# Turning the next pair's inputs inside this pair's product, in the MLP's accumulator ring

## The chip, the core and the metric

The kernel runs on one core of a Trainium2 chip. The metric is the device time of one execution in microseconds (us), the median of several runs. Before the change it is 194.65 us (three runs, 194.28 to 195.99).

The core has five engines that work side by side and wait for each other by semaphores: TensorE (matrix products and transposes, which write to PSUM, the accumulator memory), VectorE, ScalarE, GpSimd, and SyncE, which issues most transfers here. In the profile they are PE (and PEld for its weight loads), DVE, ACT, POOL and SP.

## The reference

Two stages. The first is a linear attention with decay (RWKV-5): for each of 4 batches and 8 heads a state of 48 x 48 is carried through 768 time steps. The second is an MLP with a SiLU.

```python
batch, n_heads, seq, head_dim = (4, 8, 768, 48)
for t in range(S):
    cur = np.einsum('bhd,bhe->bhde', u[None] * kt, vt)
    y[:, :, t] = np.einsum('bhd,bhde->bhe', rt, state + cur)
    state = w[None, :, :, None] * state + np.einsum('bhd,bhe->bhde', kt, vt)
# x: y as (3072, 384)
h = x @ w_in                         # 384 -> 2048
g = h * (1.0 / (1.0 + np.exp(-h)))
return (g @ w_out)                   # 2048 -> 384
```

All inputs and the output are fp32.

## The kernel before

The time axis is cut into six chunks of 128 steps. A *unit* is one chunk of one batch: 24 units, unit `i` being chunk `i // 4` of batch `i % 4`, handled in pairs `i`, `i + 1`. For each unit:

- r and k are turned (transposed) by TensorE in fp32, so that the head's 48 channels lie on the partitions, and VectorE multiplies them with powers of the decay on the way out of PSUM (`turn`, `decay`): this gives `rT` and `kT`;
- the product of `kT` and `rT` (fp32) gives a 128 x 128 matrix per head, which VectorE masks to its triangle (`masked`: `am`, fp16);
- `outputs`: `am` times v, plus `rT` times the carried state, gives `y`; k times v gives the new contribution to the state;
- `y` is evicted, turned by a DMA transpose into `xT`, and becomes input of the MLP.

The MLP is cut into small pieces, called fillers, which stand in a list and are put into TensorE's stream between the attention's steps by `fill(n)`. A piece of the first layer (`l1`) is three matmuls with 512 columns into one accumulator `hps` and a SiLU on ScalarE; a piece of the second layer (`l2`) is four matmuls with 384 columns; four such pieces fill one accumulator `ops`, which ScalarE then copies out. A chunk has 16 pieces of each layer.

PSUM holds two large tiles `att0` and `att1` (two banks each), taken in turn by the transposes and by the products, and a ring of four one-bank accumulators (tag `moe`) for everything else: `hps`, `ops`, `yp` (outputs), `sp` (state).

```python
wrk = ctx.enter_context(tc.tile_pool(name="wrk", bufs=2))
att = [ps.tile([128, 2, 512], FP, name=f"att{i}") for i in range(2)]
# ... cut ...
def turn_one(i, x):
    if x == 0:
        L(i)["t"] = next_att().rearrange("p y (x g t) -> p y x g t", x=2, g=NP)
    flat = (rin, kin)[x][i % NIN].rearrange("p h d -> p (h d)")
    for p in range(NP):
        for y in range(2):
            rows = slice(HC * y, HC * y + HC)
            nc.tensor.transpose(L(i)["t"][0:PR, y, x, p, :], flat[rows, 128 * p:128 * p + PR],
                                ident[rows, rows])

def decay_one(i, x):
    key, lam = (("rT", lamR), ("kT", lamK))[x]
    L(i)[key] = wrk.tile([PR, NP, C], FP, name=key)          # pool of two buffers
    nc.vector.tensor_tensor(
        out=L(i)[key].rearrange("p g (y t) -> p y g t", y=2),
        in0=L(i)["t"][0:PR, :, x], in1=lam.rearrange("p g (y t) -> p y g t", y=2),
        op=ALU.mult)

def product_pair(i):
    a = [next_att().rearrange("p j (g c) -> p j g c", g=NP) for _ in range(2)]
    for e in range(2):
        L(i + e)["a"] = a[e]
    for s0, c0 in ((0, 0), (HC, HC)):
        for p in range(NP):
            for e in range(2):
                rT, kT = L(i + e)["rT"], L(i + e)["kT"]
                o0 = s0 if e == 0 else HC - s0
                for j, r0 in ((0, 0), (1, 64)):
                    nc.tensor.matmul(a[e][o0:o0 + HC, j, p, c0:C],
                                     kT[r0:r0 + D, p, s0:s0 + HC],
                                     rT[r0:r0 + D, p, c0:C], start=True, stop=True)
# ... cut ...
def l1_mm(sc, b0, nb, ft):
    m = B // nb
    hps = hpss[b0, ft] = ps.tile([128, m, nb * C], FP, name="hps", tag="moe", bufs=4)
    # three matmuls; then a SiLU on ScalarE

def l2_mm(sc, b, part):
    if part == 0:
        opss[b] = ps.tile([128, HD], FP, name="ops", tag="moe", bufs=4)
    # four matmuls; after part 3 a copy on ScalarE and the store
# ... cut: the head, in which the first units and MLP pieces are ordered by hand ...
load(8)
load(9)
for i in range(B + 2, NU, 2):                # B = 4, NU = 24: i = 6, 8 ... 22
    nxt = range(i + 2, min(i + 4, NU))
    product_pair(i)
    # ... cut: GpSimd's products for the next pair ...
    masked(i)
    masked(i + 1)
    fill(4)
    outputs(i)
    # ... cut: evict y, DMA transpose, state ...
    fill(2)
    outputs(i + 1)
    # ... cut: the same, and new fillers after every second pair ...
    fill(2)
    for n in nxt:
        turn(n)
        decay(n)
    load(i + B)
    load(i + 1 + B)
    for n in nxt:
        bonus_sum(n); cast_v(n); bonus_v(n); decayed_state(n)
    for n in nxt:
        fill(2)
        cast_r(n)
    fill(4)
fill(len(fillers))
```

Of the kernel before, what the change touches and what calls it, by code (L numbers as in the profile page):

```python
# [8 lines left out]
FP = mybir.dt.float32  # L9
F16 = mybir.dt.float16  # L10
AF = mybir.ActivationFunctionType
ALU = mybir.AluOpType
# [3 lines left out]
def kernel(  # L16
# [11 lines left out]
    nc = tc.nc  # L28

    B, H, S, D = r.shape  # L30
    C = 128
    NCH = S // C
    HD = H * D
    NP = H // 2
    PW = 2 * D
    PR = 64 + D
# [4 lines left out]
    NIN = 8  # L41
    HC = C // 2
# [3 lines left out]
    wrk = ctx.enter_context(tc.tile_pool(name="wrk", bufs=2))  # L46
    ps = ctx.enter_context(tc.tile_pool(name="ps", bufs=1, space=bass.MemoryType.PSUM))
    ctx.enter_context(tc.manual_schedule())

    def unit(i):  # L50
        return divmod(i, B)
# [4 lines left out]
    def next_att():  # L56
        turns.append(0)
        return att[len(turns) % 2]
# [3 lines left out]
    rin = [big.tile([128, H, 64], FP, name=f"rin{i}") for i in range(NIN)]  # L62
    kin = [big.tile([128, H, 64], FP, name=f"kin{i}") for i in range(NIN)]
# [7 lines left out]
    def ld(i, dst, src, eng=nc.sync):  # L71
        sc, b = unit(i)
        eng.dma_start(
            out=dst[i % NIN][:, :, 0:D],
            in_=src[b, :, sc * C:sc * C + C, :].rearrange("h t d -> t h d"))

    def load(i):
        if i >= NU:
            return
        for dst, src in ((rin, r), (kin, k), (vin, v)):  # L80
            ld(i, dst, src)
# [38 lines left out]
    for b in range(B):  # L120
        nc.vector.memset(st16[b], 0.0)

    ident = cst.tile([128, 128], FP)
# [10 lines left out]
        out=maskM, in_=maskM, compare_op=ALU.is_ge, fill=0.0,  # L134
# [11 lines left out]
    lamR = cst.tile([PR, NP, C], FP)  # L146
    lamK = cst.tile([PR, NP, C], FP)
# [54 lines left out]
    def L(i):  # L202
        return live.setdefault(i, {})

    def bonus_products(i):
        bonus_ku(i)
        bonus_rku(i)
# [10 lines left out]
    def decayed_k(i):  # L218
        nc.gpsimd.tensor_tensor(out=kc[i % NIN][:, :, 0:D], in0=kin[i % NIN][:, :, 0:D],  # L219
                                in1=lamC, op=ALU.mult)  # L220

    def bonus_sum(i):
        L(i)["rku"] = wrk.tile([128, H], FP, name="rku")
        nc.vector.tensor_reduce(out=L(i)["rku"], in_=L(i)["rku_f"],  # L224
                                axis=mybir.AxisListType.X, op=ALU.add)

    def bonus_v(i):
        L(i)["vu"] = wrk.tile([128, H, D], FP, name="vu")
        nc.gpsimd.tensor_tensor(out=L(i)["vu"], in0=vin[i % NIN],  # L229
                                in1=L(i)["rku"].unsqueeze(2).broadcast_to([128, H, D]),  # L230
                                op=ALU.mult)

    def crossed(i):
        return i % 2 == 1
# [9 lines left out]
# [12 lines that stand above are left out]
        L(i)[key] = wrk.tile([PR, NP, C], FP, name=key)  # L256
# [5 lines that stand above are left out]
    def turn(i):  # L262
        turn_one(i, 0)
        turn_one(i, 1)

    def decay(i):
        decay_one(i, 0)
        decay_one(i, 1)
# [3 lines left out]
        nc.scalar.copy(out=L(i)["rT16"], in_=L(i)["rT"])  # L272

    def product_pair(i):
        a = [next_att().rearrange("p j (g c) -> p j g c", g=NP) for _ in range(2)]
        for e in range(2):
            L(i + e)["a"] = a[e]
        for s0, c0 in ((0, 0), (HC, HC)):
            for p in range(NP):
                for e in range(2):  # L280
                    rT, kT = L(i + e)["rT"], L(i + e)["kT"]
                    o0 = s0 if e == 0 else HC - s0
                    for j, r0 in ((0, 0), (1, 64)):
                        nc.tensor.matmul(a[e][o0:o0 + HC, j, p, c0:C],  # L284
                                         kT[r0:r0 + D, p, s0:s0 + HC],
                                         rT[r0:r0 + D, p, c0:C],
                                         start=True, stop=True)

    def masked(i):
        am = L(i)["am"] = wrk.tile([128, 2, NP, C], F16, name="am")  # L290
        nc.vector.tensor_tensor(  # L291
            out=am.rearrange("p h g c -> p (h g) c"), in0=L(i)["a"].rearrange("p h g c -> p (h g) c"),
            in1=(maskX if crossed(i) else maskM).unsqueeze(1).broadcast_to([128, H, C]), op=ALU.mult)
# [27 lines left out]
    def outputs(i):  # L321
        outputs_y(i)
        outputs_s(i)

    def decayed_state(i):
        sc, b = unit(i)
        if 0 < sc < NCH - 1:
            L(i)["sdec"] = wrk.tile([PR, NP, PW], FP, name="sdec", bufs=4)
            nc.gpsimd.tensor_tensor(out=L(i)["sdec"], in0=st[b],  # L329
                                    in1=wCT.unsqueeze(2).broadcast_to([PR, NP, PW]), op=ALU.mult)  # L330

    def evict_y(i):
        L(i)["y16"] = wrk.tile([128, H, D], F16, name="y16")
        nc.vector.tensor_tensor(out=L(i)["y16"], in0=L(i)["y"], in1=L(i)["vu"], op=ALU.add)  # L334

    def state(i):
        sc, b = unit(i)
        if sc == NCH - 1:
            return
        sps = L(i)["sps"]  # L340
        for p0, c0 in ((0, 0), (64, D)):
            dst = st[b][p0:p0 + D, :, c0:c0 + D]
            src = sps[p0:p0 + D, :, c0:c0 + D]
            if sc:
                nc.vector.tensor_tensor(out=dst, in0=src,
                                        in1=L(i)["sdec"][p0:p0 + D, :, c0:c0 + D], op=ALU.add)
            else:
                nc.vector.tensor_copy(out=st16[b][p0:p0 + D, :, c0:c0 + D], in_=src)
                nc.vector.tensor_copy(out=dst, in_=src)
# [13 lines left out]
    def turn_y_dma(i):  # L363
        sc, b = unit(i)
        nc.sync.dma_start_transpose(out=x_tile(sc)[:, :, b, :],
                                    in_=L(i)["y16"].rearrange("p h d -> p (h d)"))
# [31 lines left out]
    def l1(sc, b0, nb, ft):  # L398
        l1_mm(sc, b0, nb, ft)
        l1_silu(sc, b0, nb, ft)  # L400
# [22 lines left out]
            store(sc, b)  # L423

    fillers = []

    def fill(n):
        for _ in range(n):
            if fillers:
                fillers.pop(0)()  # L430
# [45 lines left out]
    for word in order.split():  # L476
        if "*" in word:
            n, word = word.split("*")
# [10 lines left out]
            l1(1, 0, 2, 2 * int(word[1]))  # L489
        else:  # L490
            unit_steps[word[:-1]](int(word[-1]))
    load(8)
    load(9)
    fillers.extend([lambda ft=ft: l1(1, 0, 2, ft) for ft in range(10, NFT, 2)])
    fillers.extend(second(0))

    for i in range(B + 2, NU, 2):
        sc, b = unit(i)
        nxt = range(i + 2, min(i + 4, NU))
        product_pair(i)  # L500
        if i > B + 2:
            for n in nxt:
                bonus_products(n)
                decayed_k(n)
        if i > B + 2:
            masked(i)
            masked(i + 1)
        else:
            bonus_v(i)
            decayed_k(i)  # L510
            decayed_state(i)
            masked(i)
            bonus_sum(i + 1)
            masked(i + 1)
            bonus_v(i + 1)
            decayed_k(i + 1)
            decayed_state(i + 1)
            for n in nxt:
                bonus_products(n)
                decayed_k(n)  # L520
        fill(4)
        outputs(i)
        evict_y(i)
        turn_y_dma(i)
        state(i)
        state16(i)
        fill(2)
        outputs(i + 1)
        evict_y(i + 1)
        turn_y_dma(i + 1)  # L530
        state(i + 1)
        state16(i + 1)
        if b:
            fillers.extend((first(sc) if sc > 1 else rest_first(sc)) + second(sc))
        fill(2)
        for n in nxt:
            turn(n)
            decay(n)
        load(i + B)
        load(i + 1 + B)  # L540
        for n in nxt:
            bonus_sum(n)
            cast_v(n)
            bonus_v(n)
            decayed_state(n)
        for n in nxt:
            fill(2)
            cast_r(n)
        fill(4)
    fill(len(fillers))  # L550


# [28 lines left out]
```

## Time and profile before

The profiled execution has a span of 195.2 us. In the groups below a line such as L284 is a line of the kernel; then come the engine, the operation, the tiles (written <- read), the shape and how many there are, the busy time and the mean of one instruction.

| what | engine | number | mean |
|---|---|---|---|
| product `att<-rT,kT` (L284) | TensorE, fp32 | 768 | 258 ns |
| first layer `hps<-xT,win` (L387) | TensorE, fp16 | 360 | 337 ns |
| second layer `ops<-wout,gT` (L408) | TensorE, fp16 | 384 | 326 ns |
| decay `rT<-att,lamR`, `kT<-att,lamK` (L257) | VectorE | 24 + 24 | 685 and 683 ns |
| mask `am<-att` (L291) | VectorE | 12 + 12 | 1225 and 1215 ns |
| SiLU `gT<-hps` (L395) | ScalarE | 96 | 598 ns |
| cast `rT<-rT` (L272) | ScalarE | 20 | 619 ns |

Matmuls overlap in TensorE's pipeline, so their mean is a latency; what one costs in a stream is the distance between starts. Each product matmul is recorded twice[...]. Transposes are the instructions of L251.

### The profile page before, as it was taken

How to read it: one execution, taken by the hardware profiler on the slowest of the kernel's cores; microseconds unless marked ns; L12 is line 12 of the kernel's file. 1: busy time of each engine (PE TensorE's matmuls, PEld its weight loads, DVE VectorE, ACT ScalarE, POOL GpSimd, SP SyncE). 2: the span in 40 equal slices, each digit the busy share in tenths (PEclk: the TensorE clock that was granted, in tenths of full speed). 3: DMA queues.
4: the chain of work that ended last, by engine and by line, in shares of the span. 5: the costliest groups of instructions: out<-in, count | busy, mean ns of one | idle time of the engine just before them, and what ended most of it. 6: DMA issues, size and time to landing. Idle time of an engine off the chain costs nothing.

```text
span 195.2 us, 5592 instructions
## 1 busy us (share of the span) xinstructions
PE 186.8 (96%) x2290; PEld 119.4 (61%) x2290; DVE 102.9 (53%) x188; ACT 108.2 (55%) x211; POOL 120.3 (62%) x159
## 2 busy tenths in 40 slices
PE   7998999889999999999999999999999999999992
PEld 2565676567766786665556655566655657644561
DVE  6348869783862772782782673663564364200121
ACT  5394558749563384076793186791386781089200
POOL 8567994999999948919919829839837430000000
PEclk9999999999999999999999999999999999999999
DMA  5999999999748639258349269168287201310022
GB/s 95 210 205 179 201 167 176 172 211 190 109 100 164 186 75 232 69 113 177 90 95 211 64 146 195 30 125 181 61 185 162 43 1 44 95 66 0 6 78 81
DMA packets 90123, 24.35 MB, mean 125 GB/s; under 512 B 83313, under 2 KB 90098, under 8 KB 90098
## 3 DMA queue, kind: packets, MB, share of 16 engines
q1 hardware_dynamic: 84992, 20.46, 48.1%
q0 software_dynamic: 3712, 3.15, 11.1%
q10 hardware_dynamic: 1394, 0.40, 0.8%
q8 instruction: 18, 0.29, 0.7%
q14 instruction: 7, 0.06, 0.1%
HBM read 20.65 MB, written 4.72 MB: 130 GB/s over the span
## 4 chain that ended last, share of the span: by engine, by line
PE 75%; POOL 13%; issue 4%; DMA 2%; ACT 2%; DVE 1%; ACTq 0%; POOLq 0%
PE ops L408 32%; PE hps L387 26%; PE att L284 7%; PE att L251 4%; POOL ku L211 3%; POOL kc L219 3%; POOL vu L229 2%; DMA u_bc<-in_u_dram 2%; POOL rku_f L215 2%; PE yp L306 2%; PE yp L301 2%; POOL win L84 2%; PE sp L318 1%; ACT gT L395 1%; POOL sdec L329 0%
## 5 line engine op out<-in xcount | busy, mean ns | idle before, releaser
L387 PE MATMUL hps<-xT,win 128*128 128x512 f16 (+1 forms) x360 | 68.2, 337 | 0.7 <-ACT xT L376 0.5
L395 ACT ACTIVATE gT<-hps 128x512 f16<-128x512 f32 x96 | 56.2, 598 | 19.9 <-PE hps L387 17.8
L408 PE MATMUL ops<-wout,gT 128*128 128x384 f16 x384 | 66.6, 326 | 0.0
L408 PEld LDWEIGHTS <-gT 128*128 128x128 f16 x384 | 36.2, 98 | 23.2
L387 PEld LDWEIGHTS <-win 128*128 128x128 f16 x360 | 33.2, 98 | 24.2 <-issue 1.1
L229 POOL TENSOR_TENSOR vu<-vin,rku 128x384 f32<-128x384 f32 x24 | 19.8, 830 | 29.9 <-DVE rku L224 29.9
L414 ACT COPY osb<-ops 128x384 f32<-128x384 f32 x20 | 9.6, 479 | 43.4 <-PE ops L408 43.4
L291 DVE TENSOR_TENSOR am<-att,maskM 128x1024 f16<-128x1024 f32 x12 | 14.7, 1225 | 35.0 <-PE att L284 35.0
L211 POOL TENSOR_TENSOR ku<-kin,u_bc 128x384 f32<-128x384 f32 x24 | 24.1, 1005 | 3.5 <-DMA u_bc<-in_u_dram 2.3
L215 POOL TENSOR_TENSOR rku_f<-rin,ku 128x384 f32<-128x384 f32 x24 | 24.1, 1003 | 1.7
L219 POOL TENSOR_TENSOR kc<-kin,lamC 128x384 f16<-128x384 f32 x24 | 23.9, 1000 | 0.0
L284 PEld LDWEIGHTS att<-rT,kT 48*64 48x64 f32 x768 | 18.9, 141 | 6.5 <-issue 3.9
L257 DVE TENSOR_TENSOR rT<-att,lamR 112x512 f32<-112x512 f32 x24 | 16.4, 685 | 11.5 <-ACT gT L395 4.0
L284 PE MATMUL att<-rT,kT 48*64 48x128 f32 (+1 forms) x768 | 21.4, 258 | 0.8 <-DVE rT L257 0.8
L334 DVE TENSOR_TENSOR y<-yp,vu 128x384 f16<-128x384 f32 x24 | 13.3, 556 | 13.7 <-issue 4.8
L257 DVE TENSOR_TENSOR kT<-att,lamK 112x512 f32<-112x512 f32 x24 | 16.4, 683 | 3.6 <-PE att L251 3.5
L291 DVE TENSOR_TENSOR am<-att,maskX 128x1024 f16<-128x1024 f32 x12 | 14.6, 1215 | 0.0
L416 DVE COPY osb<-ops 128x384 f32<-128x384 f32 x4 | 2.2, 558 | 21.8 <-PE ops L408 21.8
L329 POOL TENSOR_TENSOR sdec<-st,wCT 112x384 f32<-112x384 f32 x16 | 13.2, 826 | 0.0
L238 ACT CAST v<-vin 128x384 f16<-128x384 f32 x24 | 11.4, 511 | 3.2 <-DMA vin<-in_v_dram 3.2
L224 DVE TENSOR_REDUCE rku<-rku_f 128x8 f32<-128x384 f32 x24 | 12.4, 544 | 0.8 <-POOL rku_f L215 0.7
L272 ACT CAST rT<-rT 112x512 f16<-112x512 f32 x20 | 12.4, 619 | 0.3 <-DVE rT L257 0.2
(60 smaller groups left out, 167.0 us busy)
## 6 DMA issues: line engine op xcount, KB each, us to landing
rin<-in_r_dram SPq DMA_DIRECT2D x24, 192.0 KB, 4.1
vin<-in_v_dram SPq DMA_DIRECT2D x24, 192.0 KB, 3.9
out_dram<-osb SPq DMA_DIRECT2D x24, 192.0 KB, 2.2
kin<-in_k_dram SPq DMA_DIRECT2D x23, 192.0 KB, 4.1
win<-in_moe_w_in_dram POOLq DMA_DIRECT2D x4, 384.0 KB, 6.3
wout<-in_moe_w_out_dram POOLq DMA_DIRECT2D x4, 384.0 KB, 6.5
xT<-y SPq DMA_TRANSPOSE x18, 2.3
kin<-in_k_dram ACTq DMA_DIRECT2D x1, 192.0 KB, 3.7
```

The costliest lines, as they stand in the source:

```text
L211: nc.gpsimd.tensor_tensor(out=L(i)["ku"], in0=kin[i % NIN][:, :, 0:D], in1=u_bc, op=ALU.mult)
L215: nc.gpsimd.tensor_tensor(out=L(i)["rku_f"], in0=rin[i % NIN][:, :, 0:D], in1=L(i)["ku"], op=ALU.mult)
L219: nc.gpsimd.tensor_tensor(out=kc[i % NIN][:, :, 0:D], in0=kin[i % NIN][:, :, 0:D], in1=lamC, op=ALU.mult)
L229: nc.gpsimd.tensor_tensor(out=L(i)["vu"], in0=vin[i % NIN], in1=L(i)["rku"].unsqueeze(2).broadcast_to([128, H, D]), op=ALU.mult)
L257: nc.vector.tensor_tensor(out=L(i)[key].rearrange("p g (y t) -> p y g t", y=2), in0=L(i)["t"][0:PR, :, x], in1=lam.rearrange("p g (y t) -> ...
L284: nc.tensor.matmul(a[e][o0:o0 + HC, j, p, c0:C], kT[r0:r0 + D, p, s0:s0 + HC], rT[r0:r0 + D, p, c0:C], start=True, stop=True)
L291: nc.vector.tensor_tensor(out=am.rearrange("p h g c -> p (h g) c"), in0=L(i)["a"].rearrange("p h g c -> p (h g) c"), in1=(maskX if crossed ...
L329: nc.gpsimd.tensor_tensor(out=L(i)["sdec"], in0=st[b], in1=wCT.unsqueeze(2).broadcast_to([PR, NP, PW]), op=ALU.mult)
L334: nc.vector.tensor_tensor(out=L(i)["y16"], in0=L(i)["y"], in1=L(i)["vu"], op=ALU.add)
L387: nc.tensor.matmul(hps[:, f, :], win[:, q, (ft + f) * 128:(ft + f + 1) * 128], xts[sc][:, q, b0:b0 + nb, :].rearrange("p b t -> p (b t)"), ...
L395: nc.scalar.activation(out=gts[sc][:, ft:ft + m, b0 * C:(b0 + nb) * C], in_=hpss[b0, ft], func=AF.Silu)
L408: nc.tensor.matmul(opss[b], gts[sc][:, ft, b * C:(b + 1) * C], wout[:, ft, :], start=(ft == 0), stop=(ft == NFT - 1))
```

## The change

The loop's pairs from `i = 8` on take another order.

- The transposes of the next pair stand between the two halves of this pair's product, so that product and transposes form one stretch of fp32 work on TensorE.
- They no longer use `att0` and `att1`, which the product occupies, but all four accumulators of the MLP's ring: each unit's transposes go to two tiles, one for each half of the chunk's 128 steps (`turn_halves`), and the decays become four per unit with half the elements each (`decay_halves`).
- The decays stand before the masks in VectorE's order.
- The number of MLP pieces of each pair is set by a table: 8 and 24 in turn in place of 16 (15 in the first, 16 in the second, 20 in the next to last). The pieces around the transposes are then those of the second layer, which take one ring buffer for four pieces.
- Loads run two units further ahead.

```diff
+    def turn_halves(i):
+        L(i)["th"] = [ps.tile([128, 512], FP, name="th", tag="moe", bufs=4)
+                      .rearrange("p (x g t) -> p x g t", x=2, g=NP) for _ in range(2)]
+        for x in range(2):
+            flat = (rin, kin)[x][i % NIN].rearrange("p h d -> p (h d)")
+            for p in range(NP):
+                for y in range(2):
+                    rows = slice(HC * y, HC * y + HC)
+                    nc.tensor.transpose(L(i)["th"][y][0:PR, x, p, :],
+                                        flat[rows, 128 * p:128 * p + PR], ident[rows, rows])
+
+    def decay_halves(i):
+        for key in ("rT", "kT"):
+            L(i)[key] = wrk.tile([PR, NP, C], FP, name=key)
+        for y in range(2):
+            for x, (key, lam) in enumerate((("rT", lamR), ("kT", lamK))):
+                t0 = HC * y
+                nc.vector.tensor_tensor(
+                    out=L(i)[key][:, :, t0:t0 + HC], in0=L(i)["th"][y][0:PR, x],
+                    in1=lam[:, :, t0:t0 + HC], op=ALU.mult)
... cut: product_pair split into open_products and products(i, s0) ...
+    STEPS = {6: 15, 8: 16, 10: 8, 12: 24, 14: 8, 16: 24, 18: 8, 20: 20, 22: 8}
...
-    load(8)
-    load(9)
+    for i in range(8, 12):
+        load(i)
...
-        product_pair(i)
-        if i > B + 2:
+        ahead = i > B + 2
+        if ahead:
+            open_products(i)
+            products(i, 0)
+            for n in nxt:
+                turn_halves(n)
+            products(i, HC)
             for n in nxt:
                 bonus_products(n)
                 decayed_k(n)
-        if i > B + 2:
+            for n in nxt:
+                decay_halves(n)
             masked(i)
             masked(i + 1)
+            fill(6)
         else:
+            product_pair(i)
... cut: the first pair keeps its order and its fill(4) ...
-        fill(2)
-        for n in nxt:
-            turn(n)
-            decay(n)
-        load(i + B)
-        load(i + 1 + B)
+        if not ahead:
+            fill(2)
+            for n in nxt:
+                turn(n)
+                decay(n)
+        load(i + 6)
+        load(i + 7)
... cut ...
+        left = STEPS[i] - 8
         for n in nxt:
-            fill(2)
+            if left > 4:
+                fill(2)
+                left -= 2
             cast_r(n)
-        fill(4)
+        fill(left)
```

It is meant to save TensorE one change between fp16 and fp32 work and back in every pair, and to take the decays out of the stretch behind the outputs.

More of the change, by code (lines that the diff above doesn't have):

```diff
@@ L274, in product_pair, with open_products @@
     def product_pair(i):
-        a = [next_att().rearrange("p j (g c) -> p j g c", g=NP) for _ in range(2)]
+        open_products(i)
+        products(i, 0)
+        products(i, HC)
+    def open_products(i):
         for e in range(2):
-            L(i + e)["a"] = a[e]
-        for s0, c0 in ((0, 0), (HC, HC)):
-            for p in range(NP):
[L280 to L287, printed above, removed]
+            L(i + e)["a"] = next_att().rearrange("p j (g c) -> p j g c", g=NP)
@@ new lines, in products @@
+    def products(i, s0):
+        for p in range(NP):
+            for e in range(2):
+                rT, kT = L(i + e)["rT"], L(i + e)["kT"]
+                o0 = s0 if e == 0 else HC - s0
+                for j, r0 in ((0, 0), (1, 64)):
+                    nc.tensor.matmul(L(i + e)["a"][o0:o0 + HC, j, p, s0:C],
+                                     kT[r0:r0 + D, p, s0:s0 + HC], rT[r0:r0 + D, p, s0:C],
+                                     start=True, stop=True)
+    def turn_halves(i):
[3 more added lines that the diff above has]
+            flat = (rin, kin)[x][i % NIN].rearrange("p h d -> p (h d)")
+            for p in range(NP):
+                for y in range(2):
+                    rows = slice(HC * y, HC * y + HC)
+                    nc.tensor.transpose(L(i)["th"][y][0:PR, x, p, :],
+                                        flat[rows, 128 * p:128 * p + PR], ident[rows, rows])
@@ L499 @@
         nxt = range(i + 2, min(i + 4, NU))
-        product_pair(i)
-        if i > B + 2:
+        ahead = i > B + 2
+        if ahead:
+            open_products(i)
+            products(i, 0)
+            for n in nxt:
+                turn_halves(n)
+            products(i, HC)
             for n in nxt:
@@ L520 @@
                 decayed_k(n)
-        fill(4)
+            fill(4)
         outputs(i)
@@ L545 @@
             decayed_state(n)
+        left = STEPS[i] - 8
         for n in nxt:
-            fill(2)
+            if left > 4:
+                fill(2)
+                left -= 2
             cast_r(n)
-        fill(4)
+        fill(left)
     fill(len(fillers))
```

## The prediction

> **What bounds the kernel now.** I read the engine totals first, then the chain of work that ended last, then the chain inside one steady pair.
>
> ```profile
> span 195.2 us, 5592 instructions
> PE 186.8 (96%) x2290; PEld 119.4 (61%) x2290; DVE 102.9 (53%) x188; ACT 108.2 (55%) x211; POOL 120.3 (62%) x159
> PEclk9999999999999999999999999999999999999999
> ```
>
> TensorE is busy 96% of the span at its full clock; no other engine passes 62%. Busy matmul time alone proves little, so I asked the chain where it runs between two products (start, length, what):
>
> ```profile
> 104.72 1.50 PE att L284 x64
> 106.22 2.71 PE ops L408 x16
> ...
> 109.31 0.17 PE sp L318 x4
> 109.48 1.30 PE ops L408 x8
> ...
> 111.16 0.17 PE sp L318 x4
> 111.33 1.30 PE ops L408 x8
> 112.63 1.04 PE att L251 x32
> 113.67 2.06 PE ops L408 x12
> 115.72 3.24 PE hps L387 x15
> ```
>
> Every piece starts where the one before it ends, and all are TensorE's. So in the steady loop nothing but TensorE sets the time: whatever makes it wait is added to the total, and whatever shortens its own stream is taken off. The next product starts at 118.96, so a pair of units takes 118.96 - 104.72 = 14.24 us.
>
> The price of a change of type stands in the same lines. ops x8 takes 1.30, i.e. 0.163 us per matmul; x12 after the transposes takes 2.06 where 12 x 0.163 = 1.95. So leaving an fp32 block costs about 0.11 us. The individual matmul starts of the trace agree and add the entry: the last fp16 matmul's stream ends 0.09 us before the first fp32 matmul starts, the second fp32 group comes about 0.05 late, and after the last fp32 one the first fp16 matmul starts 0.15 us later, where its row's own rhythm is 0.06 (transposes) or 0.04 (second half of the product). A block so costs about 0.24 us beyond its own work, and a pair has two: product and transposes.
>
> VectorE between two products (start, length, what, idle before):
>
> ```profile
> 106.27 1.22 DVE L291 TENSOR_TENSOR am<-att,maskM 128x1024 f16<-128x1024 f32 x1 [3.78 <-PE att L284]
> 107.41 1.21 DVE L291 TENSOR_TENSOR am<-att,maskX 128x1024 f16<-128x1024 f32 x1
> 113.33 0.69 DVE L257 TENSOR_TENSOR rT<-att,lamR 112x512 f32<-112x512 f32 x1 [0.89 <-ACT v L238]
> 113.94 0.68 DVE L257 TENSOR_TENSOR kT<-att,lamK 112x512 f32<-112x512 f32 x1
> ```
>
> The four decays of a pair stand far from the product, with ops pieces to run meanwhile; starts are 0.60 us apart for 512 elements, 1.14 for 1024.
>
> [...]from the trace's own 685 (512) and 1215 (1024) the slope is 1.04 ns per element, and 256 comes to 0.42 as well.
>
> **The change part by part.** Seven pairs (i = 8 to 20) have a next pair and run the new branch; i = 6 keeps the old one and i = 22 has nothing to turn.
>
> 1. One fp32 block for two. Seven times an entry and an exit go: 0.24 us each. The merged block has two inner switches (product to transposes and back, another shape of weights), which I take at 0.03 us each. Gain 7 x 0.18 = **-1.3 us**.
>
> 2. The wait that replaces them. The four turned tiles (two units by two halves) are all four buffers of the accumulator ring. The first MLP piece after the block, always an ops piece of a new accumulator, therefore can't start until the two decays that read the first of them are done. And these can't start when the transposes are: rT and kT lie in a pool of two buffers each, which hold the pair whose product is still running. The decay of unit i+2 overwrites rT of unit i, so it waits for unit i's last product matmul, at the very end of the block. The compiled order of the changed kernel bears this out: the decay waits for TensorE, the mask after it needs no TensorE wait of its own any more, and the ops weight load after the block waits for VectorE. So putting the transposes inside the product hides nothing. Chain from the start x of the last product matmul: x + 0.27 VectorE starts (before: last start at 106.00, mask at 106.27); + 0.33 for the distance to the second decay (0.60 less 256 x 1.04 ns); + 0.42 for its length; + 0.05 until TensorE runs (in the head of the kernel a decay ends at 46.89 + 0.68 = 47.57 and the product starts at 47.63). x + 1.07, where fp16 now starts at x + 0.15. TensorE stands still for 0.91 us, seven times: **+6.4 us**.
>
> 3. Eight half decays for four. 8 x 0.33 = 2.7 us for 2.4, then the masks. If the block's fp16 would have started at P, the decays run from P + 0.12 to P + 2.8 and the masks end at P + 4.0 and P + 5.1. Six pieces of 0.65 us now stand before the outputs, from P + 0.91 to P + 4.8; the second output comes at P + 6.7. Both masks are in time. **0**.
>
> 4. The long pairs (24 pieces: i = 12, 16, 20). Twelve hps pieces follow each other after the second output, while ScalarE has v's casts and two casts of rT in its queue before and between their SiLUs. Its starts in the trace: 127.38 first cast, 129.38 first SiLU after them, then 0.49 per SiLU or cast when it is behind. TensorE's ring lets it run four pieces ahead. The fifth hps needs the first SiLU's end; putting the two rows beside each other gives stops of about 0.2 us at the fifth, seventh and ninth piece, then ScalarE (0.49) overtakes TensorE (0.65). About 0.55 us, three times: **+1.7 us**. Before, only three hps pieces followed those casts, and no stop shows.
>
> 5. The short pairs (8 pieces: 10, 14, 18) take about 9.9 us. GpSimd needs 2 x (3 x 1.0 + 0.83 + 0.83 + 0.5) = 10.3 us per pair, but has 20 us in the long pair after it, and its products are wanted half a pair later. VectorE needs some 10 us, also only once in two pairs. The second unit's turned tiles need the last state update, which ends about 0.2 us before. **0**, with a risk of a few tenths.
>
> 6. Loads two units deeper. Six more loads stand on the queue before the loop, where the DMA is full (share above 1 from 30 to 50 us), and compete with the last piece of w_out, which landed at 52.4 and is wanted at about 54. I allow **+0.3 us**. The number of MLP pieces and the tail after the last output stay.
>
> Sum: -1.3 + 6.4 + 1.7 + 0.3 = +7.1 us on 194.65: about 201.7 us.
>
> **The rivals.** (a) The merged block is all there is: the waits of step 2 are hidden, as the change intends, and the time is 193.3 us. For it: the transposes finish half a product earlier, and the order of pieces was plainly chosen with care. Against it: the two-buffer pool, which leaves VectorE nothing it may write before the product ends. (b) Only step 2 happens, and ScalarE keeps up: 194.65 - 1.3 + 6.4 = 199.8 us. For it: before, ScalarE idles 17.8 us in total waiting for hps. Against: those are pairs with the casts far from a row of hps. (c) The short pairs are bound by VectorE or GpSimd (10 us each against 9.9): every short pair then loses up to a microsecond more, 203 to 205 us. Against it: neither result is wanted at once. (d) w_out arrives late behind the additional loads: up to 1.5 us, once.
>
> **Range and chances.** Step 2 is the large term; its inputs are measured, and I trust it to 0.15 us per pair, 1 us in all. Step 4 may be 0 to 2.5, step 1 -0.4 to -1.7, steps 5 and 6 together 0 to 2. I predict 201.5 us, with 198.3 to 204.0 for 8 in 10. Slower by over 2% begins at 198.5: chance 0.86. Within 2%: 0.11. Faster by over 2% would need 190.8, more than every type switch in the loop is worth: 0.03.
>
> **What would show it.** Right: seven idle stretches of about 0.9 us on TensorE in front of ops, released by the half decays of kT; decays starting about 0.27 us after the last product matmul's start and not after the transposes; a merged block of about 2.5 us; in long pairs, waits of hps for SiLU. Wrong: decays that run during the second half of the product, ops that follow the block after 0.15 us, or a total under 197 us. If TensorE is idle in the block's middle, waiting for ring buffers or loads, a wait that I put at nothing was the larger one.

## The result, and the profile after

| kernel | median | ratio, 95% interval |
|---|---|---|
| before | 194.91 us (6 runs) | |
| changed | 204.70 us (6 runs) | 1.0511 (1.0467 to 1.0555) |

The change costs 9.8 us. Slower by over 2% was forecast; the time lies 0.7 us above the predicted range.

The totals of the changed kernel's page, as those shown of before:

```profile
span 203.0 us, 5641 instructions
PE 185.1 (91%) x2290; PEld 117.5 (58%) x2290; DVE 104.5 (51%) x216; ACT 106.3 (52%) x211; POOL 120.4 (59%) x159
```

TensorE does the same 2290 matmuls in about the same busy time; its share falls from 96% to 91%. So the time went into waiting rather than into work. The chain that ended last, around the block of pair `i = 14` (start, length, what):

```profile
105.95 1.03 PE att L289 x32
106.98 1.04 PE th L301 x32
108.02 0.69 PE att L289 x32
...
108.75 0.16 DVE rT L310
...
109.09 0.42 DVE kT L310
...
109.56 4.07 PE ops L433 x24
```

Before, this chain was TensorE alone. Now it leaves TensorE behind the product, runs through two half decays on VectorE and comes back with the first MLP piece. VectorE's own list (start, length, what, idle before) shows where those decays stand:

```profile
108.75 0.42 DVE L310 TENSOR_TENSOR rT<-th,lamR 112x256 f32<-112x256 f32 x1 [11.61 <-PE att L289]
109.09 0.41 DVE L310 TENSOR_TENSOR kT<-th,lamK 112x256 f32<-112x256 f32 x1
...
111.41 1.21 DVE L316 TENSOR_TENSOR am<-att,maskM 128x1024 f16<-128x1024 f32 x1
```

VectorE was idle for 11.6 us, and what releases it is the product (`att`), not the transposes (`th`), which TensorE had left at 108.02. The list of who waited for whom (us in total, times, longest) counts it over the kernel; of before, none of these three lines exists:

```profile
PE ops L433 <- DVE kT L310: 6.4, 7, 0.9
PE ops L433 <- DMA wout<-in_moe_w_out_dram: 0.5, 1, 0.5
PE hps L412 <- ACT gT L420: 0.2, 1, 0.2
```

The third line is small because the profile counts only idle time there, and matmuls overlap: an hps matmul of 512 columns lasts 379 ns in the record, and the next one starts 216 ns after it did. The chain shows these stops in the long pair ahead of that block (`i = 12`):

```profile
94.99 2.59 PE hps L412 x12
97.61 1.46 PE hps L412 x6
99.11 1.46 PE hps L412 x6
100.60 2.75 PE hps L412 x12
```

Six hps matmuls take 1.30 us in a stream. Their starts in the trace are 0.42 us apart instead of 0.22 at three places: ahead of the fifth, the seventh and the ninth piece after the outputs.

To compare traces without the head of the kernel, whose length differs from execution to execution by more than 1 us (the first load of w_out is issued at 36.0 us in the trace of before, and at 33.6 in that of the run on shape and type, which has the same head), I take the stretch from the first product matmul of the loop (unit 6) to the start of the last matmul, called the *loop stretch* below. It is 144.38 us before and 154.39 us after, 10.0 us more. That sum can be read off in parts, each from starts of matmuls in the trace:

| part | count x us | us |
|---|---|---|
| ops waits for the decays (1.134 us from the last product matmul, where 0.151 was usual) | 7 x 0.98 | 6.9 |
| hps waits for SiLU (i = 12, 16: 3 x 0.20 each; i = 20: 0.37 + 0.20 + 0.20) | 3 pairs | 2.0 |
| ops waits for w_out, once | 1 x 0.67 | 0.7 |
| merged block against two blocks | 7 x 0.06 | 0.4 |

The last row is the surprise. Two blocks cost 2 x 0.24 us beyond their work before; one was to cost 0.24 and two inner switches. Inside the block of the profile above, the last group of the product's first half starts at 106.695 and the first transposes at 106.915, where the product's rhythm is 0.109; the next transposes come 0.05 late. Back again, 0.149 in place of 0.056, and another 0.05. The two inner switches so cost 0.15 us each, 0.30 together, although everything there is fp32: more than the 0.24 us of the entry and exit that were saved.

### The profile page after: what moved, and what is told of

It reads as the page before. It is cut to its first block, busy times and chain, and to the rows that moved or that the text cites. A ratio compares the mean times of both kernels' runs of the same rounds, so it can differ in the third digit from the quotient of the medians.

```text
span 203.0 us, 5641 instructions
## 1 busy us (share of the span) xinstructions
PE 185.1 (91%) x2290; PEld 117.5 (58%) x2290; DVE 104.5 (51%) x216; ACT 106.3 (52%) x211; POOL 120.4 (59%) x159
## 4 chain that ended last, share of the span: by engine, by line
PE 68%; POOL 15%; DMA 7%; issue 4%; DVE 2%; ACT 2%; ACTq 0%; POOLq 0%
PE ops L433 31%; PE hps L412 22%; PE att L289 7%; DMA wout<-in_moe_w_out_dram 4%; POOL ku L211 4%; PE th L301 4%; POOL kc L219 3%; POOL rku_f L215 3%; POOL vu L229 2%; DMA u_bc<-in_u_dram 2%; PE yp L331 1%; DVE kT L310 1%; PE yp L326 1%; POOL win L84 1%; POOL wout L89 1%
## 5 line engine op out<-in xcount | busy, mean ns | idle before, releaser
L433 PE MATMUL ops<-wout,gT 128*128 128x384 f16 x384 | 65.9, 326 | 6.9 <-DVE kT L310 6.4
L420 ACT ACTIVATE gT<-hps 128x512 f16<-128x512 f32 x96 | 54.3, 609 | 10.5 <-PE hps L412 8.8
L412 PEld LDWEIGHTS <-win 128*128 128x128 f16 x360 | 33.8, 98 | 27.1 <-issue 3.9
L310 DVE TENSOR_TENSOR rT<-th,lamR 112x256 f32<-112x256 f32 x28 | 11.6, 415 | 35.6 <-PE att L289 35.6
L379 POOL CAST stb<-st 112x384 f16<-112x384 f32 x16 | 7.9, 507 | 30.1 <-DVE st L370 30.1
L289 PE MATMUL att<-rT,kT 48*64 48x128 f32 (+1 forms) x768 | 22.1, 250 | 1.0 <-DVE rT L257 0.8
L289 PEld LDWEIGHTS att<-rT,kT 48*64 48x64 f32 x768 | 17.8, 133 | 6.0 <-issue 3.3
L316 DVE TENSOR_TENSOR am<-att,maskM 128x1024 f16<-128x1024 f32 x12 | 14.6, 1216 | 11.6 <-PE att L289 11.6
```

Source lines behind the costliest of these rows:

```text
L289: nc.tensor.matmul(L(i + e)["a"][o0:o0 + HC, j, p, s0:C], kT[r0:r0 + D, p, s0:s0 + HC], rT[r0:r0 + D, p, s0:C], start=True, stop=True)
L310: nc.vector.tensor_tensor(out=L(i)[key][:, :, t0:t0 + HC], in0=L(i)["th"][y][0:PR, x], in1=lam[:, :, t0:t0 + HC], op=ALU.mult)
L316: nc.vector.tensor_tensor(out=am.rearrange("p h g c -> p (h g) c"), in0=L(i)["a"].rearrange("p h g c -> p (h g) c"), in1=(maskX if crossed ...
L412: nc.tensor.matmul(hps[:, f, :], win[:, q, (ft + f) * 128:(ft + f + 1) * 128], xts[sc][:, q, b0:b0 + nb, :].rearrange("p b t -> p (b t)"), ...
L420: nc.scalar.activation(out=gts[sc][:, ft:ft + m, b0 * C:(b0 + nb) * C], in_=hpss[b0, ft], func=AF.Silu)
L433: nc.tensor.matmul(opss[b], gts[sc][:, ft, b * C:(b + 1) * C], wout[:, ft, :], start=(ft == 0), stop=(ft == NFT - 1))
```

## The experiments

The first theory: rT and kT, with two buffers each, hold the decays back (7 x 0.98 us); v's and rT's casts before a row of SiLUs cause the hps stops (2.0 us); the deeper loads cause the stop at w_out; a switch between transposes and product costs what a switch of type costs. Where a theory of a run below says "before", it is the time of the kernel before beside it on the same chip.

### Four buffers for rT and kT

```diff
-        L(i)[key] = wrk.tile([PR, NP, C], FP, name=key)
+        L(i)[key] = wrk.tile([PR, NP, C], FP, name=key, bufs=4)
```

(in both places where they are made)

> The changed kernel with four buffers for rT and kT in place of two, nothing else. Theory (the two-buffer pool holds the decays back until the product's end): the decays start about 0.27 us after the first unit's transposes, ops follows the block after some 0.15 us in place of 1.13, seven times 0.98 = 6.9 us go, 197.8 us (197.2 to 198.6). Rival (the accumulator ring itself: four turned tiles fill it, and no decay is done early enough to free one): decays start earlier but ops still waits 0.5 us or more, 201 us or more.

Measured: 199.32 us beside 195.6 for the kernel before, ratio 1.0155 (1.0102 to 1.0209); loop stretch 147.96 us, 6.4 less than the changed kernel. VectorE and TensorE at the block of `i = 14`:

```profile
105.51 0.42 DVE L310 TENSOR_TENSOR rT<-th,lamR 112x256 f32<-112x256 f32 x1 [10.14 <-PE th L301]
```

```profile
105.46 0.39 PE L301 MATMUL th<-ident,kin 64*112 64x64 f32 x8
105.78 0.69 PE L289 MATMUL att<-rT,kT 48*64 48x64 f32 x32
106.41 0.82 PE L433 MATMUL ops<-wout,gT 128*128 128x384 f16 x4
```

Now the transposes (`th`) release the decays, while they and the second half of the product still run, and ops follows without a stop. So the pool of two held them, and the ring alone does not. In absolute time the run is over the expected range, since the kernel before was slower beside it, by 0.7 us, and because three of the seven stops do not go wholly: in the pairs after a short one (`i` = 12, 16, 20) 0.37 us each stays (ops starts 0.52 us after the last product matmul). VectorE's list at `i = 16` shows what stands ahead of the decays:

```profile
114.50 0.54 DVE L224 TENSOR_REDUCE rku<-rku_f 128x8 f32<-128x384 f32 x1
115.08 0.42 DVE L310 TENSOR_TENSOR rT<-th,lamR 112x256 f32<-112x256 f32 x1
```

VectorE is still at the bonus sums of the short pair. That this is what delays them is tested by the run with 12 and 20 pieces. The backlog lay hidden under the larger wait. 6.9 + 0.67 (w_out, no stop in this trace) - 3 x 0.37 = 6.5; the loop stretch has 6.4.

### Transposes ahead of the product

```diff
-            products(i, 0)
             for n in nxt:
                 turn_halves(n)
+            products(i, 0)
             products(i, HC)
```

(with four buffers)

> As the one with four buffers, with the transposes ahead of the whole product instead of inside it. Theory (each change between transposes and product costs about 0.15 us although both are fp32): one inner change fewer, 7 x 0.15 = 1.0 us less, 196.8 us. Rival (only the change of type costs, the distances of starts inside the block are an artefact): the same as four buffers inside the product, within 0.3 us.

Measured: 200.17 us, ratio 1.0226 (1.0158 to 1.0294). Neither came: it is slower than with the transposes inside. In the three pairs after a short one, the second unit's transposes need the ring buffer of the last state, whose eviction VectorE has not done: a stop of 0.67 us, which standing inside the product had hidden. In the other four pairs they wait 0.14 us for a copy of ScalarE, as in the section "The same with the transposes first" below. The run doesn't tell the two theories of the switch apart; the test of shape and type below does.

### v's and rT's casts moved to behind the block

```diff
+            for n in nxt:
+                cast_v(n)
+                cast_r(n)
             masked(i)
             masked(i + 1)
             fill(6)
```

(with four buffers for rT and kT, and for rT16; the casts leave their old place)

> As the one with four buffers, with ScalarE's casts of v and rT moved from behind the outputs to just behind the block, where it has only ops copies (four buffers for rT16 too). Theory (the casts in front of twelve SiLUs make the ring run dry in the long pairs): the stops of 0.2 us at hps go, 0.6, 0.6 and 0.8 us in three pairs, 195.8 us. Rival (ScalarE is too slow for sixteen SiLUs in a row anyway): the stops stay, 197.5 us or more.

Measured: 197.35 us, ratio 1.0082 (1.0055 to 1.0109); loop stretch 145.84 us, 2.1 less than with four buffers alone. All nine stops at hps are gone, so ScalarE is fast enough for sixteen SiLUs in a row (when it is behind, its SiLUs start 0.49 us apart; a piece of hps takes TensorE 0.65); the casts ahead of them were the cause. ScalarE's list of the changed kernel shows the queue that was undone:

```profile
94.96 0.92 ACT L238 CAST v<-vin 128x384 f16<-128x384 f32 x2
95.91 0.51 ACT L241 COPY vx<-v 64x384 f16<-64x384 f16 x1
...
96.97 1.09 ACT L420 ACTIVATE gT<-hps 128x512 f16<-128x512 f32 x2
97.94 0.62 ACT L272 CAST rT<-rT 112x512 f16<-112x512 f32 x1
98.45 1.10 ACT L420 ACTIVATE gT<-hps 128x512 f16<-128x512 f32 x2
```

The first SiLU of the row starts 2.0 us after the casts began, and after two of them another cast stands in the queue; the hps pieces stop at 97.4, 98.9 and 100.4.

### The deeper loads alone

```diff
-    load(8)
-    load(9)
+    for i in range(8, 12):
+        load(i)
...
-        load(i + B)
-        load(i + 1 + B)
+        load(i + 6)
+        load(i + 7)
```

(in the kernel before)

> The kernel before with only its loads two units deeper (units 8 to 11 before the loop, i+6 and i+7 in it). Theory (the six loads more before the loop delay the third piece of w_out, TensorE stops once for 0.67 us): 195.5 us, w_out lands after 52 us and ops waits for it once. Rival (that stop is chance of one execution): 194.9 us, no wait of ops for w_out.

Measured: 195.76 us, ratio 1.0021 (0.9984 to 1.0058): no difference that this resolves. The last w_out piece took 8.6 us to land (6.6 before, 9.0 changed), and ops started some 0.25 us late once. But three of the other traces with the deeper loads show no late start at all, and the next experiment, which has the old loads, shows one of 0.44 us:

```profile
52.19 0.97 PE L419 MATMUL ops<-wout,gT 128*128 128x384 f16 x5 [0.28 <-DMA wout<-in_moe_w_out_dram]
```

In the kernel before, the piece landed at 52.36 and TensorE came to it at 54.15; in the changed kernel it landed no later, at 52.12, but TensorE came at 51.49. So the stop at w_out can't be laid to the deeper loads; it depends on how soon TensorE gets there.

### Shape or type

Two changes happen at once where an MLP piece meets the product: fp16 to fp32, and matmuls of the whole array (128 x 128) to matmuls on corners of it (48 rows x 64 columns). This run separates them, in the kernel before, with extra matmuls whose results are overwritten or masked away.

```diff
     def product_pair(i):
... cut: the two accumulators
+        if i >= 8 and i % 4 == 0:
... cut: 16 fp16 matmuls, rT16 with itself, 48 rows x 64 columns, in the four corners
+        elif i >= 8:
... cut: 4 fp32 matmuls, ident with ident[:, 0:64], whole array
```

> The kernel before with extra matmuls ahead of eight products, whose results the product or its mask discards: in pairs 8, 12, 16, 20 sixteen fp16 matmuls in the product's own tile shape (48 rows, 64 columns, in the four corners), in pairs 10, 14, 18, 22 four fp32 matmuls of the whole array (128 x 128, 64 columns[...]). So a change of tile shape and a change of type stand apart. Theory (a change of tile shape costs about 0.15 us in distances of starts beyond the rhythm, whatever the types): fp16 whole array to fp16 corners shows it and fp16 corners to fp32 corners doesn't; fp16 whole to fp32 whole doesn't and fp32 whole to fp32 corners does. Rival (the type costs): the reverse in all four places.

Measured: the rows of TensorE, first in pair 12 (start, length, what, tile, shape, type), then in pair 10:

```profile
88.24 1.24 PE L398 MATMUL hps<-xT,win 128*128 128x512 f16 x5
89.42 0.32 PE L281 MATMUL att<-rT 48*64 48x64 f16 x16
89.56 0.96 PE L295 MATMUL att<-rT,kT 48*64 48x128 f32 x28
```

```profile
73.59 0.81 PE L419 MATMUL ops<-wout,gT 128*128 128x384 f16 x4
74.24 1.00 PE L285 MATMUL att<-ident 128*128 128x64 f32 x8
75.17 0.56 PE L295 MATMUL att<-rT,kT 48*64 48x128 f32 x12
```

| from, to | changes | distance of starts | rhythm |
|---|---|---|---|
| hps fp16 whole, fp16 corners | shape | 0.309, then 0.053 | 0.216, then 0.031 |
| fp16 corners, product fp32 corners | type | 0.032, then 0.139 | 0.031, then 0.109 |
| ops fp16 whole, fp32 whole | type | 0.163 | 0.163 |
| fp32 whole, product fp32 corners | shape | 0.205, then 0.160 | 0.112, then 0.109 |

(The rhythm is the distance of starts, or of groups of four in corners, within one row of equal matmuls; each of the four whole-array fp32 matmuls has two records, hence x8; the first of the whole-array fp32 distances is 0.056, all later ones 0.112.) What goes beyond the rhythm is 0.11 and 0.14 us at a change of shape; at a change of type it is nothing in one case and 0.03 in the other. The theory of shape holds in all four rows, and the rival in none.

The weight loads show the same border. At the same two places (start, length, what):

```profile
89.41 0.21 PEld L281 LDWEIGHTS <-rT 48*64 48x64 f16 x16 [0.42 <-issue]
89.53 0.86 PEld L295 LDWEIGHTS att<-rT,kT 48*64 48x64 f32 x32
```

```profile
74.08 1.02 PEld L285 LDWEIGHTS att<-ident 128*128 128x128 f32 x8
75.17 0.42 PEld L295 LDWEIGHTS att<-rT,kT 48*64 48x64 f32 x16
```

Where only the type changes, the first load starts ahead of its matmul, while older matmuls still run (89.53 for 89.56, 74.08 for 74.24). Where the shape changes, it starts with its matmul (89.41 for 89.42, 75.17 for 75.17). In the loops of five traces (before, changed, this run and the last two below) every such change of shape has the load at most 0.005 us ahead, and every other border between two rows of matmuls at least 0.02. Between the whole array and 112 rows x 128 columns, as the outputs alternate, the load stays 0.023 to 0.045 us ahead (before and changed) and nothing beyond the rhythm is seen (0.042 us from a matmul of 96 columns to the next, on 112 rows as on 128), so that is no change of shape in this sense. That the late load is what costs the time is not shown by itself.

Transposes use 64 rows x 112 columns, the product 48 x 64: another shape. Standing in one fp32 stretch saves nothing, since each inner border is a change of shape too. The single time of this run, 199.53 us, says nothing of the change, as it contains the extra matmuls.

### 12 and 20 pieces, with early casts

```diff
-    STEPS = {6: 15, 8: 16, 10: 8, 12: 24, 14: 8, 16: 24, 18: 8, 20: 20, 22: 8}
+    STEPS = {6: 15, 8: 16, 10: 12, 12: 20, 14: 12, 16: 20, 18: 12, 20: 16, 22: 8}
```

> As the one with four buffers and early casts, with 12 and 20 pieces per pair in place of 8 and 24. Theory (after a short pair VectorE is still at the last state and the sums of the bonus when the turned tiles are ready, so three of the seven decays start late, 0.37 us each): with four pieces more in the short pair those stops go, loop 1.1 us shorter, ratio to before 1.002. Rival (the three stops come from the ring, not from VectorE's backlog): they stay, ratio 1.008.

Measured: 199.24 us, ratio 1.0221 (1.0170 to 1.0273): slower, and yet the stops of 0.37 us went, as the theory of VectorE's backlog has it. Three new ones of 0.9 us came, at the fifth hps behind the block. ScalarE's list there:

```profile
88.53 0.62 ACT L272 CAST rT<-rT 112x512 f16<-112x512 f32 x1 [1.92 <-DVE rT L310]
...
90.66 0.62 ACT L272 CAST rT<-rT 112x512 f16<-112x512 f32 x1
91.18 1.56 ACT L420 ACTIVATE gT<-hps 128x512 f16<-128x512 f32 x3
```

With 12 and 20 pieces, hps stands right behind the block, and its SiLUs stand behind rT's casts, which wait for the decays. Both statements, on VectorE's backlog and on the cast, were tested by the last run.

### The same with the transposes first

> The same with the transposes ahead of the whole product. Theory (one change of shape fewer per pair, and no late state to wait for): 7 x 0.15 = 1.0 us less than inside the product, ratio to before 0.997. Rival (transposes first wait for the ring, as in the short pairs of the version with 8 and 24): ratio 1.005 or more.

Measured: 195.73 us, ratio 1.0046 (1.0019 to 1.0072): over 0.997 and just under the rival. There are no stops at SiLU, as the decays are done earlier. But the gain of 0.15 us per pair from one change of shape less isn't there: two pairs take 11.74 + 16.90 = 28.64 us, where two pairs before take 28.47. The starts show why (ScalarE, then TensorE):

```profile
101.96 0.48 ACT L439 COPY osb<-ops 128x384 f32<-128x384 f32 x1 [2.00 <-PE ops L433]
102.35 0.58 PE L301 MATMUL th<-ident,rin 64*112 64x64 f32 x8
```

The second of these eight transposes, the first into the last of the four tiles, starts at 102.50, where usually it follows the first after 0.004 us. It waits for its ring buffer, which the last `ops` accumulator holds until ScalarE's copy ends at 102.44. In all seven pairs it starts 0.045 us after the signal of that copy, and the transposes end 0.14 us late. So the rival was right in its mechanism: a wait for the ring takes what the saved change of shape gives. Inside the product, TensorE comes to the transposes later, and no such break is seen.

### No stop left

```diff
+            for n in nxt:
+                cast_v(n)
             masked(i)
             masked(i + 1)
             fill(6)
```

(four buffers, 12 and 20 pieces; rT's casts at their old place)

> Four buffers for rT and kT, 12 and 20 pieces, v's casts early, but rT's casts where the changed kernel has them, between the last pieces. Theory (with 12 and 20 pieces and all casts early, rT's cast stands in front of the SiLUs and itself waits for the decays; that alone made the new stop of 0.9 us): no stop of 0.1 us or more in the loop, two pairs take 28.6 us against 28.47 before, 0.4 us more in all, and up to 0.7 for w_out: ratio 1.002 to 1.006. Rival (the ring of four is too short for eight hps behind the block): stops at hps stay, ratio over 1.01.

Measured: 195.98 us, ratio 1.0034 (0.9994 to 1.0074). The windows of two pairs (length, then busy time of TensorE, its weight loads, VectorE, ScalarE, GpSimd):

```profile
85.92:102.80 16.88, 16.88 (x194) 9.62 (x193) 8.36 (x18) 12.25 (x23) 14.78 (x19) 1.00 0.75 152
102.80:114.50 11.70, 11.70 (x177) 8.10 (x176) 8.36 (x18) 4.32 (x9) 5.29 (x7) 1.00 0.37 97
```

TensorE never stops: its busy time fills both windows. The two pairs take 28.58 us against 28.47 before (14.23 and 14.24). The loop stretch is 144.74 us against 144.38: 0.36 us more, seven times 0.05. This is the change without its waits, and nothing of the intended gain is in it: 0.05 us per pair is what two inner changes of shape cost beyond the entry and exit saved. No version tried is faster than the kernel before.

## Why the prediction was wrong

It said 201.5 us, 6.9 over its 194.65 (its own sum gives 7.1); measured were 9.8 over 194.91. Direction and main cause were right, the size was 2.9 us short.

- **Step 1, one fp32 block for two: wrong, and it is the step that failed.** It took the two inner switches "at 0.03 us each", because it held the change of type to be what costs. The separate test puts the cost on the change of the matmul's shape on the array; the inner switches measure 0.15 us each. In place of -1.3 us stands +0.4, outside the -0.4 to -1.7 that it allowed for this step: 1.7 us of the 2.9. The price of 0.24 us per block was read rightly; but at each border it was read from, shape and type change together.
- **Step 2, the wait for the decays: mechanism right.** Seven stops, released by kT's half decay, and four buffers take them away. The term was mis-sized by 0.5 us: 0.98 in place of 0.91 us per pair. VectorE starts 0.32 us after the last product matmul's start (0.27 predicted), the second decay follows after 0.34 (0.33), and a half decay takes 0.415 (0.42).
- **Step 3, the masks: right.** They end before the outputs; no wait for a mask stands in the loop.
- **Step 4, the long pairs: right in place and cause, 2.0 us in place of 1.7.** The stops are at the fifth, seventh and ninth piece. In i = 20 the first is 0.37 us.
- **Step 5, the short pairs: right for this kernel.** The backlog of VectorE that it named is there, and costs 3 x 0.37 us only once the larger wait in front is taken away.
- **Step 6, w_out: the stop came, 0.67 us in this trace for 0.3.** Its cause was argued wrongly, so that it came at all was luck: a kernel with the old loads shows such a stop too, and the loads alone change the time by less than the interval.

Of the rivals, (a) would have needed step 1 as it was predicted and no step 2; the version without any stop shows that even then there is no gain. (b) fell with the nine hps stops, (c) didn't occur, and (d) came with 0.7 us, under step 6.

The gap at the block's end repeated in seven pairs, and its own row pointed to the full PSUM ring: ops waits 6.4 us in all for kT's half decays, which free it. But the buffers that were missing were those of rT and kT, one step further up: with four of them the waits on that row are 0.9 us.

## What to carry to other kernels

Before work is moved ahead of a step, look at which buffers its result is written to: if the step still reads them, the move hides nothing until the pool is deeper (6.4 us of waits here, 0.9 with four buffers). When a border between two kinds of matmul shows a cost, test shape and type apart before grouping by one of them; here two groups of equal type but different tile shape still had the border. And moving small pieces between pairs shifts the other engines' queues too: a row of SiLUs and the casts of the same engine belong into different stretches (here 2.0 us while they shared one).

## What was not expected of the hardware

- On TensorE, a change from matmuls of the whole array to 48 x 64 corners, or between 64 x 112 and 48 x 64 parts, cost 0.11 to 0.15 us here; fp16 to fp32 at the same shape cost 0.00 to 0.03 us.
- Sixteen fp16 matmuls of 48 rows x 64 columns in the four corners, in the run on shape and type, started in groups of four, a group every 0.031 us.
- At each of these changes of shape, the next weight load started with its matmul (at most 0.005 us ahead); at other borders of the loop it started at least 0.02 us ahead, under the matmuls before.
